# One-by-one release of row scatters, and a new order of loads, ranks and clears, in an attention and expert-layer kernel

## The chip, the cores and the metric

The kernel runs on one core of one Trainium2 chip. The metric is the device time of one execution, in microseconds (us). The core's engines are TensorE (PE, matrix products, with its weight loads shown as PEld), VectorE (DVE), ScalarE (ACT), GpSimd (POOL) and SyncE (SP, which issues most DMA transfers). Each works through its own queue of instructions in order, and semaphores tie the queues together.

## The reference

Linear attention with decay over batch 4, 8 heads, 768 positions, 64 values per head, and then a layer of 8 experts of which each row uses one:

```python
intra = (q_block @ k_block.T) * Dmask      # per block of positions
inter = (q_block * lam_pow) @ kv_state
kv_state = lam_block * kv_state + (k_block * rev_pow).T @ v_block
x = attn_out.transpose(0, 2, 1, 3).reshape(B * S, H * D)     # 3072 rows of 512
logits = x @ w_gate + modality_bias[modality_id]
e_idx = argmax(logits)                     # one expert for each row
h = relu(x[mask] @ w1[e])                  # 512 to 1024
out[mask] = gate_w[mask] * (h @ w2[e])     # 1024 to 512
```

All data is float32. With these inputs the rows go to four of the eight experts: 1319 to expert 3, 1494 to expert 6, 253 to expert 5 and 6 to expert 7.

## The kernel before

**Attention.** The kernel walks the positions in 24 blocks of 128, taken in 12 pairs m = 0 to 11 (a pair's data, 2048 KB, is one `load`). For a block, `scores` are matmuls of keys and queries (L251), `mask` multiplies them by the decay on DVE (L256), `keys` makes the decayed keys `kd` on ACT (L233, for the first two blocks on POOL), `query` makes `qd` on POOL (L218), `products` multiply `kd` with the values (L264), `add` brings them into the state on DVE (L274), `from_state` multiplies `qd` with the state (L286), and `values` adds the masked scores times the values (L294) and copies the sum to `xt` on ACT (L298). `scores` and `keys` of a pair are made ahead, in the iteration before it. After every second pair `turns` transposes four blocks' results into rows (L312 on PE, L316 on DVE, L318 on ACT) and `gates` makes the logits (L323).

**Routing.** The 24 blocks form three batches of eight. `choose` finds each row's expert on DVE, `ranks` (L375 to L378, PE) counts the rows ahead of it, `slots_of` turns that into a place, and for each block `one_slot` copies its tags (L406) and scatters the 128 rows into a DRAM table `placed` (L407, both on POOL). `count` (L436) and the lists of tiles follow, in DVE operations that are queued up by `put` (all at L348) and emitted by `do`, between other work. Scatters wait in a list of `jobs`. `go` issues some at a given place, `tick` issues one that waits for a given matmul to finish, and `need` issues what is left. In the attention part the table `aside` says how many are issued in pairs 6, 7, 8, 10 and 11, at two places each; from the second tile on `first_layer` and `second` call `tick` on their matmuls.

**Experts.** The rows are fetched back in tiles of 256 (tiles 0 to 3 from lists that are made early, then a tile of 64 and one of 32 rows, then eight further full ones; nine more are conditional and are not run with these inputs). A matrix is split into a high part (ACT, L596) and a low part (DVE, L597) and a product is the sum of three matmuls (L693 to L695). `first_layer` makes `hh` and `hl`, `second` the output, which ACT scales (L741) and POOL scatters to the result (L744). The low parts `w2l` of a tile are made during its own `first_layer`. The two small tiles use unsplit products (`thin_first`, L765) and turn the result (`thin_turn`, L776). The weights of the second of them are loaded into tiles of their own, `both1` and `both2`; other weights go to `raw1` and `raw2`. Rows past the end of an expert's part of `placed` are cleared by `clear_end` on SP, in two DMAs for each expert, of 64 rows always and of 192 rows if needed (two of the eight are, here).

**What sets the order.** PE, DVE, ACT and SP run their instructions in the order of the code; on POOL the order is tied together by `pool`. SP issues in that order too, and a load waits there until its target is free, so what stands behind it waits as well.

Of the kernel before, what the change touches and what calls it, by code (L numbers as in the profile page):

```python
# [15 lines left out]
P = 128  # L16
# [27 lines left out]
def linear_attention_moe(tc, qkv, lam, modality, wg, mbias, w1, w2, out):  # L44
    nc = tc.nc
    with ExitStack() as ctx:
# [28 lines left out]
        nc.scalar.dma_start(out=lamh, in_=lam.rearrange("h o -> (h o)").partition_broadcast(P))  # L75
# [170 lines left out]
        def scores(g):  # L246
            kt, qt, vt, kn = loaded(g)
            scs[g] = ps.tile([P, 2, NP, P], F32, name="s", bufs=2)
            for p in range(NP):
                for hl, r in enumerate(halves2):  # L250
                    mm = nc.tensor.matmul(scs[g][:, hl, p, :], kt[r, p, :], qt[r, p, :], start=True, stop=True)  # L251
                    begun.setdefault(g, mm)

# [35 lines left out]
        def values(g):  # L289
            c = g % NC  # L290
            vt, op, pt = loaded(g)[2], ops.pop(g), pts.pop(g)
            for p in range(NP):
                for hl in range(2):
                    nc.tensor.matmul(op[place(g, hl), p, :], vt[:, (2 * p + hl) * D : (2 * p + hl + 1) * D],  # L294
                                     pt[:, hl, p, :], start=(c == 0 and p == 0), stop=(p == NP - 1))
            if g % 4 == 0:
                xts[g // 4] = work.tile([P, NP, 4, 4, Q], F32, name="xt", bufs=2)
            nc.scalar.copy(out=xts[g // 4][:, :, :, ORDER.index(g % 4), :], in_=op.rearrange("p a (c t) -> p a c t", c=4))  # L298

# [20 lines left out]
        def gates(grp):  # L320
            for p in range(NP):
                for t in range(4):
                    nc.tensor.matmul(lps[t * Q : (t + 1) * Q, grp % 2, :], wgq[:, ORDER[t] % HB, p, :], xts[grp][:, p, :, t, :],  # L323
                                     start=(p == 0), stop=(p == NP - 1), tile_position=(0, t * Q))

        def turns(grp):
            turn(grp, 0)
            turn(grp, 1)
            gates(grp)
            turn(grp, 2)  # L330
            turn(grp, 3)

# [174 lines left out]
        def late_list(exA, nA):  # L507
# [10 lines left out]
            put(nc.vector.tensor_copy, out=ends_at[:, 0, :], in_=beyond)  # L518
# [4 lines left out]
            def first_of(those, nm):  # L523
# [18 lines left out]
            put(nc.vector.scalar_tensor_tensor, out=ends_at[:, 1, :], in0=rem, scalar=0.0, in1=thins, op0=ALU.not_equal,  # L542
                op1=ALU.subtract)
# [92 lines left out]
        def clear_end(e):  # L636
            vr = nc.sync.value_load(ends_at[0:1, 0, e : e + 1], min_val=0, max_val=E * CAP - TT)
            for i in range(2):
                if i == 0:
                    c = clear(bass.ds(vr, XT), XT)  # L640
                else:
                    cr = nc.sync.value_load(ends_at[0:1, 1, e : e + 1], min_val=0, max_val=1)
                    c = clear(bass.ds(vr + XT, TT - XT), TT - XT, cond=cr)
                apart("ends", c)
                for b in range(RN):
                    tc.declare_no_dep(c.ins, group=f"slots{b}", reason="rows differ")
                for b in range(2):
                    tc.declare_no_dep(c.ins, group=f"list{b}", reason="rows differ")
# [76 lines left out]
        behind = []  # L725

        def second(n, t, ticks=(1, 3, 5, 7), hold=False):
# [9 lines left out]
            if hold:  # L737
                y = const.tile([P, DM], F32, name="held")
            else:
                y = work.tile([P, DM], F32, name="y", tag="qd", bufs=4)  # L740
            nc.scalar.activation(out=y, in_=yp, func=AF.Copy, scale=idx[:, t, 1:2].bitcast(F32))  # L741

            def store():
                sc = nc.gpsimd.indirect_dma_start(  # L744
                    out=out, out_offset=bass.IndirectOffsetOnAxis(ap=idx[:, t, 0:1], axis=0),
                    in_=y, in_offset=None, bounds_check=N - 1, oob_is_err=False)
                apart("tokens", sc)
                pool(sc, free=True)

            if hold:  # L750
                behind.append(store)
            else:
                store()
# [60 lines left out]
        ends_at = const.tile([P, 2, E], I32, name="ends_at")  # L814
# [22 lines left out]
        aside = {6: (0, 3), 7: (1, 2), 8: (1, 1), 10: (2, 2), 11: (2, 2)}  # L837

        def block(g, on_pool=False):
            scores(g)  # L840
            mask(g)
            keys(g, on_pool)
            query(g)

# [275 lines left out]
```

## Time and profile before

| | us |
|---|---|
| median of three runs | 424.59 (420.89 to 424.86) |
| profiled execution | 424.69 |
| its span | 423.0 |
| PE busy | 393.4 (93%) |
| DVE busy | 261.9 (62%) |
| ACT busy | 211.1 (50%) |
| POOL busy | 96.8 (23%) |

The span is the profiled stretch; the execution's time holds 1.7 us more. Times in the rows are from the span's start. A timeline row merges instructions of one line that follow each other; "x32" is their number, and the bracket is the idle time before the first of them with what ended it ("issue" is an idle time that nothing in the profile explains).

### The profile page before, as it was taken

What the parts mean: (1) busy time and instruction counts of PE and PEld (TensorE: products, weight loads), DVE (VectorE), ACT (ScalarE), POOL (GpSimd) and SP (SyncE); (2) the same over time, 40 slices, a digit from 0 to 9 for tenths busy, and PEclk for the clock granted to TensorE, in tenths of its full rate; (3) what the DMA queues carried; (4) which work ended last, traced back from release to release, by engine and by line L of the source; (5) the groups of instructions that cost most, each with busy time, mean ns of one, the idle gap of its engine ahead of it and who ended that gap; (6) DMA issues with size and microseconds to landing.
All of it is one profiled execution on the core that took longest, in us unless ns stands there. A gap on an engine that the chain in (4) does not pass through costs nothing.

```text
span 423.0 us, 9783 instructions
## 1 busy us (share of the span) xinstructions
PE 393.4 (93%) x3602; PEld 343.9 (81%) x3602; DVE 261.9 (62%) x478; ACT 211.1 (50%) x411; POOL 96.8 (23%) x126
## 2 busy tenths in 40 slices
PE   6999999896898999999958999999999999999993
PEld 3879888785786888989833899989898989898982
DVE  4557779767468368787221766667666675847530
ACT  1458677574165345555120655464646555546420
POOL 1643217536400167001000102020201010010201
PEclk9999999999798999999997999999999999999998
DMA  6998896989537978125169227787403021210101
GB/s 239 389 404 304 329 339 220 394 272 286 202 101 218 302 265 266 51 53 175 24 173 341 44 51 247 213 242 224 98 24 77 25 51 51 51 51 2 52 2 48
DMA packets 37962, 72.96 MB, mean 172 GB/s; under 512 B 7054, under 2 KB 19854, under 8 KB 37904
## 3 DMA queue, kind: packets, MB, share of 16 engines
q1 hardware_dynamic: 33840, 59.45, 45.2%
q0 software_dynamic: 3920, 12.78, 7.9%
q8 instruction: 30, 0.49, 0.5%
q14 instruction: 28, 0.23, 0.2%
q10 hardware_dynamic: 144, 0.00, 0.0%
HBM read 90.57 MB, written 17.84 MB: 256 GB/s over the span
## 4 chain that ended last, share of the span: by engine, by line
issue 48%; PE 35%; POOL 6%; DVE 5%; DMA 3%; ACT 2%; POOLq 1%; DVEq 0%; ACTq 0%
POOL out_dram L744 5%; PE o L294 5%; PE s L251 5%; PE kv L264 3%; PE o L286 3%; PE o L695 3%; PE o L693 3%; PE o L694 3%; PE o L312 3%; PE s L713 2%; DMA lamh<-in_lam_dram 1%; DVE grp L316 1%; DMA out_dram<-y,idx 1%; PE kv L693 1%; ACT kd L233 1%
## 5 line engine op out<-in xcount | busy, mean ns | idle before, releaser
L597 DVE TENSOR_TENSOR w2l<-raw,w2h 128x1024 fp32r<-128x1024 f32 x48 | 58.8, 1224 | 42.3 <-ACT w2h L596 41.4
L744 POOL DMA_INDIRECT out_dram<-y,idx x23 | 29.1, 1263 | 228.0 <-ACT y L741 228.0
L695 PE MATMUL o<-w2h,hl 128*128 128x512 f32 x192 | 75.6, 394 | 0.0
L693 PE MATMUL o<-w2h,hh 128*128 128x512 f32 x192 | 75.5, 393 | 0.0
L694 PE MATMUL o<-w2l,hh 128*128 128x512 f32 x192 | 75.4, 393 | 0.0
L597 DVE TENSOR_TENSOR w1l<-raw,w1h 128x1024 fp32r<-128x1024 f32 x44 | 51.7, 1220 | 2.4 <-ACT w1h L596 2.3
L695 PE MATMUL kv<-xh,w1l 128*128 128x256 f32 x176 | 50.0, 284 | 0.0
L695 PE MATMUL s<-xh,w1l 128*128 128x256 f32 x176 | 50.0, 284 | 0.0
L596 ACT CAST w2h<-raw 128x1024 fp32r<-128x1024 f32 x48 | 49.9, 1040 | 0.1
L694 PE MATMUL s<-xl,w1h 128*128 128x256 f32 x176 | 49.9, 284 | 0.0
L694 PE MATMUL kv<-xl,w1h 128*128 128x256 f32 x176 | 49.9, 283 | 0.0
L693 PE MATMUL s<-xh,w1h 128*128 128x256 f32 x176 | 49.6, 282 | 0.0
L693 PE MATMUL kv<-xh,w1h 128*128 128x256 f32 x176 | 49.5, 281 | 0.0
L596 ACT CAST w1h<-raw 128x1024 fp32r<-128x1024 f32 x44 | 42.8, 1045 | 0.0
L695 PEld LDWEIGHTS o<-w2h,hl 128*128 128x128 f32 x192 | 36.3, 189 | 7.7
L694 PEld LDWEIGHTS o<-w2l,hh 128*128 128x128 f32 x192 | 36.5, 190 | 7.4
L693 PEld LDWEIGHTS o<-w2h,hh 128*128 128x128 f32 x192 | 36.5, 190 | 7.3
L741 ACT ACTIVATE y<-o,idx 128x512 f32<-128x512 f32 x23 | 15.8, 685 | 43.5 <-PE o L695 37.9
L233 ACT ACTIVATE kd<-load,dk 128x64 f32<-128x64 f32 x144 | 35.5, 336 | 0.1
L218 POOL TENSOR_TENSOR qd<-load,pq 128x512 f32<-128x512 f32 x20 | 25.2, 1276 | 44.3 <-PE s L251 20.5
L693 PEld LDWEIGHTS kv<-xh,w1h 128*128 128x128 f32 x176 | 33.4, 190 | 1.7 <-ACT hh L720 1.7
L693 PEld LDWEIGHTS s<-xh,w1h 128*128 128x128 f32 x176 | 33.3, 189 | 0.6 <-issue 0.2
(208 smaller groups left out, 663.8 us busy)
## 6 DMA issues: line engine op xcount, KB each, us to landing
raw<-in_w_dram SPq DMA_DIRECT2D x104, 512.0 KB
load<-in_qkv_dram SPq DMA_DIRECT2D x9, 2048.0 KB
xg<-placed SPq DMA_DIRECT2D x48, 128.0 KB
load<-in_qkv_dram SPq DMA_DIRECT2D x8, 512.0 KB
both<-in_w_dram SPq DMA_DIRECT2D x8, 512.0 KB
placed<-blank SPq DMA_DIRECT2D x8, 396.0 KB
load<-in_qkv_dram SPq DMA_DIRECT2D x2, 1024.0 KB
placed<-blank SPq DMA_DIRECT2D x8, 132.0 KB
```

The source lines that it names most:

```text
L218: op = pool(nc.gpsimd.tensor_tensor(out=qds[g], in0=loaded(g)[1], in1=pq, op=ALU.mult))
L233: nc.scalar.activation(out=kds[g][:, p, hl, :], in_=kn[:, p, hl, :], func=AF.Copy, scale=dk[:, hl, p, P - 1 : P])
L251: mm = nc.tensor.matmul(scs[g][:, hl, p, :], kt[r, p, :], qt[r, p, :], start=True, stop=True)
L264: nc.tensor.matmul(kp[r, g % HB, p, :], kd[:, p, hl, :], vt[:, (2 * p + hl) * D : (2 * p + hl + 1) * D], start=True, stop=True)
L294: nc.tensor.matmul(op[place(g, hl), p, :], vt[:, (2 * p + hl) * D : (2 * p + hl + 1) * D], pt[:, hl, p, :], start=(c == 0 and p == 0), sto ...
L596: nc.scalar.copy(out=hi, in_=src)
L597: nc.vector.tensor_tensor(out=lo, in0=src, in1=hi.bitcast(F32), op=ALU.subtract)
L693: nc.tensor.matmul(out, ah, bh, start=first, stop=False)
L694: nc.tensor.matmul(out, ah, bl, start=False, stop=False)
L695: return nc.tensor.matmul(out, al, bh, start=False, stop=last)
L741: nc.scalar.activation(out=y, in_=yp, func=AF.Copy, scale=idx[:, t, 1:2].bitcast(F32))
L744: sc = nc.gpsimd.indirect_dma_start(out=out, out_offset=bass.IndirectOffsetOnAxis(ap=idx[:, t, 0:1], axis=0), in_=y, in_offset=None, bound ...
```

## The change

1. `lamh` (the decays) is loaded through SP's queue instead of ACT's.
2. In the first pairs, block 2 is prepared whole, and block 3's keys, before block 1's results; block 4 comes before the turns of group 0, and block 5 between their halves.
3. The scatters of batches one and two no longer use `aside`. From pair 6 on, each of three places (the scores of the pair after next, the values, the gates) calls `tick`; the second batch's jobs start at pair 10 and end on the first tile's matmuls. The first fetch of rows moves from pair 8 to pair 9.
4. The third batch's `ranks` move from ahead of `second(0)` into the first quarter of tile 1's `first_layer`; its scatters, `count` and the late list follow later.
5. `clear_end` makes one DMA of 256 rows for each expert, without a condition.
6. The weights of the first small tile are issued after the clears and after the tile before it (`first_layer`), and `both1` behind the first small tile's rows instead of behind all three fetches.
7. The last output scatter is issued in its place and not behind the conditional tiles.

```diff
-        nc.scalar.dma_start(out=lamh, in_=lam.rearrange("h o -> (h o)").partition_broadcast(P))
+        nc.sync.dma_start(out=lamh, in_=lam.rearrange("h o -> (h o)").partition_broadcast(P))
...
         def clear_end(e):
-            vr = nc.sync.value_load(ends_at[0:1, 0, e : e + 1], min_val=0, max_val=E * CAP - TT)
-            for i in range(2):
-                if i == 0:
-                    c = clear(bass.ds(vr, XT), XT)
-                else:
-                    cr = nc.sync.value_load(ends_at[0:1, 1, e : e + 1], min_val=0, max_val=1)
-                    c = clear(bass.ds(vr + XT, TT - XT), TT - XT, cond=cr)
...
+            vr = nc.sync.value_load(ends_at[0:1, e : e + 1], min_val=0, max_val=E * CAP - TT)
+            c = clear(bass.ds(vr, TT), TT)
...
-            if hold:
-                behind.append(store)
-            else:
-                store()
+            sc = nc.gpsimd.indirect_dma_start(
...
         products(0)
         add(0)
-        scores(2)
-        mask(2)
-        query(2)
+        block(2)
+        keys(3)
         from_state((1,))
         values(1)
         products(1)
-        keys(2)
         add(1)
-        block(3)
+        scores(3)
+        mask(3)
+        query(3)
...
-        turns(0)
         block(4)
+        turn(0, 0)
+        turn(0, 1)
+        gates(0)
         block(5)
+        turn(0, 2)
+        turn(0, 3)
...
                 block(a + 2)
-                block(b + 2)
+                mm = block(b + 2)
+                if m > 5:
+                    tick(mm)
...
-                jobs += [("slots", one_slot)] * RC
...
+            if m == 5 or m == 10:
+                jobs += [("slots", one_slot)] * RC
             do(7)
-            go(aside.get(m, (0, 0))[0])
             from_state((a, b))
-            for g in (a, b):
-                values(g)
+            values(a)
+            mm = values(b)
+            if m > 5:
+                tick(mm)
...
-            go(aside.get(m, (0, 0))[1])
             if m % 2 and ahead:
-                turns(m // 2)
+                mm = turns(m // 2)
+                if m > 5:
+                    tick(mm)
...
                 fetch_w1(*fetch_regs(0, True))
+            elif m == 9:
+                need("slots")
                 fetch_x(0)
-            elif m == 9:
...
         def amid1(i):
             if i == 0:
                 do()
+                ranks(routed[-1])
+                slots += slots_of(*routed)
+            if i < 2:
+                do(4)
+            elif i == 2:
+                do()
                 jobs.extend([("slots", one_slot)] * RC)
-                count()
-                late_list(*early)
-            else:
-                do(4)
...
         first_layer(amid1)
+        count()
+        late_list(*early)
...
         for e in range(E):
             clear_end(e)
-        fetch_w1(*fetch_regs(thins))
+        do()
         for t in range(2):
             second(2, t)
-        do()
...
         first_layer()
-        for n in range(thins, wides + 1):
-            fetch_x(n)
+        fetch_w1(*fetch_regs(thins))
+        fetch_x(thins)
         fetch_w1(*fetch_regs(thins + 1, True), to=both1)
+        fetch_x(thins + 1)
         fetch_w2(*fetch_regs(thins))
+        fetch_x(wides)
         fetch_w2(*fetch_regs(thins + 1, True), to=both2)
```

On POOL, scatters of the first batch in pairs 6 and 7. Before, the next blocks' `qd` stand between groups of copies and scatters, which wait for no matmul (the numbers in brackets are what an instruction waits for):

```order
L407 DMA placed<-grp,sloti 26880x528 [waits Activation_49,Pool_49]
L218 TENSOR_TENSOR qd<-load,pq 128x512 [waits DMAHW4_49,PE_49]
L218 TENSOR_TENSOR qd<-load,pq 128x512 [waits PE_49]
L406 COPY grp<-pay 128x16
L407 DMA placed<-grp,sloti 26880x528 [waits Activation_49,Pool_49]
L406 COPY grp<-pay 128x16
L407 DMA placed<-grp,sloti 26880x528 [waits Activation_49,Pool_49]
L406 COPY grp<-pay 128x16
L407 DMA placed<-grp,sloti 26880x528 [waits Activation_49,Pool_49]
L218 TENSOR_TENSOR qd<-load,pq 128x512 [waits DMAHW5_49,PE_49]
```

Now each scatter waits for PE as well, and `qd` of the following blocks stands behind the scatters that are released before it:

```order
L218 TENSOR_TENSOR qd<-load,pq 128x512 [waits DMAHW4_49,PE_49]
L218 TENSOR_TENSOR qd<-load,pq 128x512 [waits PE_49]
L410 COPY grp<-pay 128x16
L411 DMA placed<-grp,sloti 26880x528 [waits PE_49,Activation_49,Pool_49]
L410 COPY grp<-pay 128x16
L411 DMA placed<-grp,sloti 26880x528 [waits PE_49,Activation_49,Pool_49]
L410 COPY grp<-pay 128x16
L411 DMA placed<-grp,sloti 26880x528 [waits PE_49,Activation_49,Pool_49]
L218 TENSOR_TENSOR qd<-load,pq 128x512 [waits DMAHW5_49,PE_49]
L410 COPY grp<-pay 128x16
L411 DMA placed<-grp,sloti 26880x528 [waits PE_49,Activation_49,Pool_49]
```

What moved is the release: a scatter starts no longer when POOL is free but when its matmul is done. The second batch's eight stand in one row in both kernels, and gain the same wait.

On PE, the passage from tile 0's first layer (L713, later L710) to its second. Before, the ranks stand between the two; the piece has the last matmuls of the first layer and the first of the ranks, then the last rank and the first of the second layer:

```order
L713 MATMUL kv_1902<-xt2_127,raw1_1390 128x256 [waits DMAHW3_49,DVE_49]
L713 MATMUL kv_1902<-xt2_127,raw1_1390 128x256 x7
L375 LDWEIGHTS lowb_106
L375 MATMUL x_124<-oh_1897,lowb_106 128x64 [waits DVE_49]
L376 LDWEIGHTS onesb_105
L376 MATMUL x_124<-ohsum_125,onesb_105 128x64
```

```order
L378 LDWEIGHTS onesb_105
L378 MATMUL x_124<-oh_1897,onesb_105 128x8
L693 MATMUL o_2034<-w2h_1789,hh0_1793 128x512 [waits PE_49,Activation_49]
L694 MATMUL o_2034<-w2l_1790,hh0_1793 128x512
L695 MATMUL o_2034<-w2h_1789,hl0_1795 128x512
```

Now the second layer follows at once, and the ranks (L379) stand behind the first quarter of the next tile's first layer:

```order
L710 MATMUL s_1874<-xt2_127,raw1_1388 128x256 x7
L710 MATMUL kv_1902<-xt2_127,raw1_1388 128x256 [waits DMAHW3_49,DVE_49]
L710 MATMUL kv_1902<-xt2_127,raw1_1388 128x256 x7
L690 MATMUL o_2015<-w2h_1777,hh0_1781 128x512 [waits DVE_49,Activation_49]
L691 MATMUL o_2015<-w2l_1778,hh0_1781 128x512
L692 MATMUL o_2015<-w2h_1777,hl0_1783 128x512
```

```order
L691 MATMUL s_2075<-xl1_131,w1h_1779 128x256
L692 MATMUL s_2075<-xh1_129,w1l_1780 128x256
L379 LDWEIGHTS lowb_106
L379 MATMUL x_124<-oh_1897,lowb_106 128x64
L380 LDWEIGHTS onesb_105
```

What moved is the wait on DVE: the first rank no longer has one here.

On SP, the end of the fetches that precede `both`. Before, the rows of the first wide tile (`xg`) and their tags stand ahead of it:

```order
L615 DMA xg<-placed 32x8x128
L615 ISA
L615 DMA xg<-placed 32x8x128
L619 ISA
L619 DMA idx_3009<-placed 128x2x2
L664 TENSOR_LOAD listC
L664 ISA x2
L672 ISA
L672 DMA both_2854<-in_w_dram 128x1024
```

Now the tags of the first small tile (`idx`) stand ahead of it, and the first wide tile's rows come after:

```order
L617 ISA
L617 DMA xq_2893<-placed 32x2x128
L624 ISA
L624 DMA idx_2892<-placed 64x2
L624 ISA
L624 DMA idx_2892<-placed 64x2
L661 TENSOR_LOAD listC
L661 ISA x2
L669 ISA
L669 DMA both_2751<-in_w_dram 128x1024
```

What moved is `both`, ahead of the fetch of the second small tile and of the first wide tile.

## Rows read from the trace of the kernel before

**Rows 1.** Page: busy us (share of the span) of each engine; GB/s in 40 equal slices.

```profile
PE 393.4 (93%) x3602; PEld 343.9 (81%) x3602; DVE 261.9 (62%) x478; ACT 211.1 (50%) x411; POOL 96.8 (23%) x126
...
GB/s 239 389 404 304 329 339 220 394 272 286 202 101 218 302 265 266 51 53 175 24 173 341 44 51 247 213 242 224 98 24 77 25 51 51 51 51 2 52 2 48
```

**Rows 2.** Waits of PE: who waited for whom: us in total, times, longest.

```profile
PE s L765 <- DMA both<-in_w_dram: 5.9, 3, 5.5
PE o L286 <- issue: 5.7, 3, 5.1
...
PE x L375 <- DVE oh L348: 1.9, 1, 1.9
...
PE x L436 <- DVE ohsum L348: 1.5, 1, 1.5
```

**Rows 3.** Windows view: stretch, length, busy us of PE, PEld, DVE, ACT, POOL, clock, DMA.

```profile
237.00:416.00 179.00, 179.00 (x1152) 163.79 (x1151) 114.25 (x123) 94.92 (x124) 21.28 (x16) 1.00 0.31 88
```

**Rows 4.** Timeline of ACT, then of PE, 16 to 32 us.

```profile
16.46 3.94 ACT L233 ACTIVATE kd<-load,dk 128x64 f32<-128x64 f32 x16
...
17.42 3.37 PE L264 MATMUL kv<-load,kd 128*64 128x64 f32 x32
...
25.03 1.07 PE L312 MATMUL o<-ident,xt 128*128 128x128 f32 x8 [0.78 <-ACT xt L298]
...
30.27 1.91 PE L264 MATMUL kv<-load,kd 128*64 128x64 f32 x16
```

**Rows 5.** Windows (pairs m = 5 and m = 7), then timeline of PE and DVE at 74 to 77.

```profile
52.75:62.21 9.46, 9.46 (x187) 8.30 (x187) 6.61 (x18) 6.55 (x24) 1.28 (x1) 1.00 0.92 324
68.16:80.46 12.30, 10.37 (x161) 8.35 (x161) 8.79 (x32) 4.84 (x16) 8.41 (x12) 1.00 0.98 350
...
74.32 0.63 PE L264 MATMUL kv<-load,kd 128*64 128x64 f32 x16
...
77.00 0.85 DVE L274 SCALAR_TENSOR_TENSOR state<-state,pq,kv 128x64 f32<-128x64 f32 x4 [2.21 <-PE o L312]
```

**Rows 6.** Timeline of DVE, PE, POOL at 93 to 107, and the stretch 104 to 112.

```profile
93.31 0.86 DVE L274 SCALAR_TENSOR_TENSOR state<-state,pq,kv 128x64 f32<-128x64 f32 x4 [1.48 <-PE kv L264]
...
101.60 0.63 PE L264 MATMUL kv<-load,kd 128*64 128x64 f32 x16
...
103.60 0.21 DVE L348 TENSOR_TENSOR deltaB<-deltaB,ntB 128x8 f32<-128x8 f32 x1
107.30 0.85 DVE L274 SCALAR_TENSOR_TENSOR state<-state,pq,kv 128x64 f32<-128x64 f32 x4 [3.49 <-remote]
...
105.08 0.98 POOL L407 DMA_INDIRECT placed<-grp,sloti  x1 [0.28 <-issue]
...
106.55 0.98 POOL L407 DMA_INDIRECT placed<-grp,sloti  x1 [0.28 <-issue]
...
104.00:112.00 8.00, 4.28 (x52) 3.98 (x54) 3.31 (x13) 0.00 (x0) 6.29 (x11) 0.57 0.87 282
```

**Rows 7.** Windows view, the stretch behind the third batch's ranks.

```profile
132.00:136.00 4.00, 4.00 (x12) 3.14 (x12) 3.09 (x5) 3.15 (x5) 0.00 (x0) 0.57 0.82 259
```

**Rows 8.** Timeline of SP, PE and ACT at the small tiles; a window of the clears.

```profile
181.13 19.83 SPq L633 DMA_DIRECT2D placed<-blank  x16
...
218.01 1.96 SPq L672 DMA_DIRECT2D both<-in_w_dram  x4
...
213.50 3.67 PE L765 MATMUL s<-raw,xf 128*64 128x256 f32 x32
...
228.92 0.66 PE L776 MATMUL x<-ident,hn 128*128 128x128 f32 x4
...
220.59 1.14 ACT L596 CAST xh<-xt 128x512 fp32r<-128x512 f32 x2 [6.30 <-DVE xt L681]
...
196.00:198.00 2.00, 2.00 (x19) 2.00 (x18) 1.28 (x2) 1.02 (x2) 0.00 (x0) 1.00 0.84 240
```

**Rows 9.** Chain that ended last: start, us, what.

```profile
412.18 4.23 DMA out_dram<-y,idx
```

More of the change, by code (lines that the diff above doesn't have):

```diff
@@ L293, in values @@
                 for hl in range(2):
-                    nc.tensor.matmul(op[place(g, hl), p, :], vt[:, (2 * p + hl) * D : (2 * p + hl + 1) * D],
-                                     pt[:, hl, p, :], start=(c == 0 and p == 0), stop=(p == NP - 1))
+                    mm = nc.tensor.matmul(op[place(g, hl), p, :], vt[:, (2 * p + hl) * D : (2 * p + hl + 1) * D],
+                                          pt[:, hl, p, :], start=(c == 0 and p == 0), stop=(p == NP - 1))
             if g % 4 == 0:
@@ L322, in gates @@
                 for t in range(4):
-                    nc.tensor.matmul(lps[t * Q : (t + 1) * Q, grp % 2, :], wgq[:, ORDER[t] % HB, p, :], xts[grp][:, p, :, t, :],
-                                     start=(p == 0), stop=(p == NP - 1), tile_position=(0, t * Q))
+                    mm = nc.tensor.matmul(lps[t * Q : (t + 1) * Q, grp % 2, :], wgq[:, ORDER[t] % HB, p, :], xts[grp][:, p, :, t, :],
+                                          start=(p == 0), stop=(p == NP - 1), tile_position=(0, t * Q))
+            return mm
         def turns(grp):
@@ L328, in turns @@
             turn(grp, 1)
-            gates(grp)
+            mm = gates(grp)
             turn(grp, 2)
             turn(grp, 3)
+            return mm
         shape = [P, RC, E]
@@ L636, in clear_end @@
         def clear_end(e):
-            vr = nc.sync.value_load(ends_at[0:1, 0, e : e + 1], min_val=0, max_val=E * CAP - TT)
-            for i in range(2):
-                if i == 0:
-                    c = clear(bass.ds(vr, XT), XT)
-                else:
-                    cr = nc.sync.value_load(ends_at[0:1, 1, e : e + 1], min_val=0, max_val=1)
-                    c = clear(bass.ds(vr + XT, TT - XT), TT - XT, cond=cr)
[L644 to L648, printed above, removed]
+            vr = nc.sync.value_load(ends_at[0:1, e : e + 1], min_val=0, max_val=E * CAP - TT)
+            c = clear(bass.ds(vr, TT), TT)
+            apart("ends", c)
+            for b in range(RN):
+                tc.declare_no_dep(c.ins, group=f"slots{b}", reason="rows differ")
+            for b in range(2):
+                tc.declare_no_dep(c.ins, group=f"list{b}", reason="rows differ")
         def thin_rows(n):
@@ L723, in first_layer, with second @@
                 between(i)
-        behind = []
-        def second(n, t, ticks=(1, 3, 5, 7), hold=False):
+        def second(n, t, ticks=(1, 3, 5, 7)):
             idx = idxs[n]
@@ L736, in second @@
                     tick(mm)
-            if hold:
-                y = const.tile([P, DM], F32, name="held")
-            else:
-                y = work.tile([P, DM], F32, name="y", tag="qd", bufs=4)
+            y = work.tile([P, DM], F32, name="y", tag="qd", bufs=4)
             nc.scalar.activation(out=y, in_=yp, func=AF.Copy, scale=idx[:, t, 1:2].bitcast(F32))
[L743 to L750, printed above, removed]
-                behind.append(store)
-            else:
-                store()
+            sc = nc.gpsimd.indirect_dma_start(
+                out=out, out_offset=bass.IndirectOffsetOnAxis(ap=idx[:, t, 0:1], axis=0),
+                in_=y, in_offset=None, bounds_check=N - 1, oob_is_err=False)
+            apart("tokens", sc)
+            pool(sc, free=True)
         def thin_first(x, w):
@@ L836, in linear_attention_moe @@
         pairs = B * NC // HB
-        aside = {6: (0, 3), 7: (1, 2), 8: (1, 1), 10: (2, 2), 11: (2, 2)}
         def block(g, on_pool=False):
-            scores(g)
+            mm = scores(g)
             mask(g)
@@ L977, in linear_attention_moe @@
         fetch_x(2)
-        ranks(routed[-1])
         turn_rows(1)
         split_rows()
-        slots += slots_of(*routed)
-        split_w1(1)
+        split_w1()
         fetch_w1(*fetch_regs(2))
@@ L1048, in linear_attention_moe @@
             for t in range(2):
-                second(n, t, hold=n + 1 == fixed_ones and t == 1)
+                second(n, t)
         ordered.close()
@@ L1064, in linear_attention_moe @@
                     second(n, t)
-        for store in behind:
-            store()
 _INS = ["qkv", "lam", "modality", "wg", "mbias", "w1", "w2"]
```

11 lines of the change are left out of this document (6 added, 5 removed).

## The prediction, made before the result was known

> **What bounds the kernel now.** I read the page's busy table first. TensorE (PE) is busy for 393.4 of 423.0 us [rows 1], so at most 29.6 us can come from its idle time, and a little more from matmuls that run at the lower clock. The view of waits, for PE, says where the large gaps are [rows 2]: 5.9 us for the weights of the small tiles (`both`), 5.7 us in three gaps before the matmuls from the state (L286), 1.9 us before the third batch's ranks (L375) and 1.5 us before a count (L436). Then I read the timeline around each, for what ended the wait. From 237 to 416 us, where the wide tiles run, the windows view shows PE busy 179.00 of 179.00 us [rows 3]: whatever is gained ahead of that arrives later only as an earlier start, and reaches the end whole.
>
> A measurement of this kernel tells about 1% (some 4 us) from no change. The sum is made against the profiled execution's own time, 424.69 us (1.7 us beyond its span), 0.1 above the median of 424.59.
>
> **First blocks.** Two blocks' `kd` on ScalarE (ACT) take 3.94 us for 16 instructions from 16.46, and the 32 products that read them take 3.37 us from 17.42: PE goes at ACT's pace [rows 4]. Sixteen products that nothing paces take 0.63 us, as those at 74.32 do [rows 5], so 32 take at most 1.26 and 2.1 us is lost. The 16 products at 30.27 take 1.91, again beside `kd`: 1.3 lost. The turn at 25.03 waits 0.78 for ACT's copy [rows 4]. Together 4.2 us. The new order issues kd(2), kd(3), kd(4) and kd(5) while PE has other work. I take 3.6 of the 4.2, since block 5's `kd` still stands near its use; bounds 2.5 and 4.5. The cover is the load: four pairs of 2.10 MB each with 0.2 MB of constants are 8.6 MB, and by the page's slices of 10.575 us at 239, 389 and 404 GB/s [rows 1] 6.6 MB has come by 21.2 us and 8.6 MB by about 26. Blocks 6 and 7, whose scores stand behind the 30.27 products at 32.1, thus have about 6 us of room: the gain is not swallowed. `lamh` on SP's queue instead of ACT's changes who issues it first: I take 0, bounds −0.5 and +0.4 (one issue, against SP having to issue it ahead of the loads).
>
> **Scatters of the first batch (m = 6 to 8).** In before, three scatters stand in a row behind the `turns` of pair m = 7's work. The products there end at 74.95, the state's update on VectorE (DVE) starts at 77.00, though its operands are there. That pair took 12.30 us where an odd pair without scatters took 9.46: 2.84 lost [rows 5]. Released one per half-pair, a scatter has its hand-over behind it. Three places a pair remain and each may still touch one hand-over, so I take 2.5; bounds 1 and 4 (the latter with what m = 8 loses).
>
> **Scatters of the second batch (m = 10, 11).** Products end at 102.23, DVE's list work at 103.81, and the update starts only at 107.30, while scatters of 0.98 us run with 0.28 us between them. Where no scatter runs, the update at 93.31 starts when its products end [rows 6]. After the change two scatters remain in this stretch and the other six move into the first tile's layer, whose matmuls wait for no such update. The update then starts behind DVE's list work at 103.9: 3.4 us gained, 1.5 us of stall left. [...]
>
> The row says that a hand-over from PE to DVE beside scatters takes 107.30 − 102.23 = 5.07 us, of which 1.58 is DVE's own list. [...]
>
> **Ranks and count of the third batch.** The ranks wait 1.9 us for DVE's `oh` ahead of `second(0)` [rows 2]. Then `second(0)` begins, and in the four us from 132 PE is busy throughout at a granted clock of 0.57 [rows 7]: 4.00 × 0.43 = 1.7 us lost. In the new place, behind the first quarter of tile 1's layer, `oh` is many us old. I gain 1.9 + 1.7 = 3.6, bounds 2.5 and 3.8. The count's 1.5 us wait on `ohsum` goes the same way: after `first_layer(1)` the DVE sums lie three steps back. I take 1.5, bounds 0.5 and 1.6. What is late next: `late_list` puts more small DVE operations (0.16 to 0.25 us each, as the one at 103.60) ahead of tile 3's layer. Some 12 of them are about 2 us on DVE, hidden because the first reader of `w2l` is `second(3)`; without that cover they cost those 2 us. The last scatters of this batch now come with `second(1)`, and the fetch of tile 3 needs only the lists' rows.
>
> **Clears and small tiles.** Before, 16 clear instructions keep SP from 181.13 to 200.96. `both` is issued at 218.01, PE ends the first small tile's layer at 217.17 and then waits for it, and the transposes at 228.92 come last. Now there are 8 clears: about half of 19.83, so SP is through at 191. They move 8 × 541 KB = 4.3 MB instead of two such and six of 135 KB. The DMA row of 196 to 198 shows 240 GB/s at a share of 0.84, or 285 GB/s full: 15.2 us, so the last byte is in by 198 [rows 8]. The first small tile's fetch waits for that, `both` is issued 3 to 6 us behind, at about 203, and its 2 MB need 7.4 us at 285 GB/s: there by 212, five before PE wants it. PE would then end the second layer at 217.17 + 3.67 = 220.8. The fetch of the first wide tile, now behind one more weight group, lands about as before, so ACT's two casts of it still run from 220.59 to 221.73, ahead of the small tile's `hn`. That one is as large as one cast, 0.57: the small tile's transposes start at about 222.4 instead of 228.92, 6.5 gained. I take 5.5, since x, weights and the last clear share the DMA engines; bounds 4 (`both` 2 us late) and 8.1 (transposes at 220.8).
>
> **End.** The last output scatter was held back behind the conditional tiles; now it is issued in its place. Its 4.23 us to landing [rows 9] remain, and what stands behind it (branches, POOL's closing row) may come before or after. I take −0.5; bounds −1.2 and +0.5.
>
> Sum: 3.6 + 2.5 + 5.5 + 3.6 + 1.5 + 5.5 − 0.5 = 21.7. 424.69 − 21.7 = 403.0 us.
>
> **Rivals.**
> A. The bunching is not the cause, or one scatter holds a hand-over as much as six: the 2.5 and 5.5 stay lost. For it: three places a pair still stand beside updates. Against it: the update at 93.31. Time 403.0 + 8.0 = 411.0. [...]
> B. The clears' 4.3 MB, in 2 KB rows, drain slower than the 285 GB/s, and the small tile's fetch comes no sooner, so `both` is no earlier. For it: clears of 135 KB are rated here beside weights, not alone. Against it: the DMA share was 0.84 with a 396 KB clear running. The small tiles bring 0 to 1: time 407.5 to 408.5.
> C. Slower: a scatter that waits for a matmul makes PE's queue answer for it, so that each of the 24 costs PE a full scatter cycle (1.47 us from one start to the next, 105.08 to 106.55 [rows 6]) at the matmul that releases it. [...] For it: POOL's order is fixed, so a `qd` behind a waiting scatter waits too. Against it: `qd` is read a pair later, and PE itself waits for no scatter here.
>
> **Chances.** Forecast 0.68 (its own range 397 to 407); A 0.12; B 0.12; C 0.03; 0.05 for less than 397, where terms reach their upper bounds. The range from 396 to 412 takes in A and B. Faster by over 1% 0.93; within 1% 0.04 (A and B together with a poor start); slower 0.03.
>
> **What would show it.** Right: the update behind the products of m = 11 starts within 2 us of their end; no PE wait at ranks and count; no half clock at those two places; `both` issued before 206 and no PE wait for it; transposes of the small tile 5 to 6 us nearer the first small layer's start than 15.4; all wides gapless. Wrong: updates that start over 2 us late beside single scatters (A); clears that end after 203 (B); gaps at the releasing matmuls (C); a new wait for a load among the first eight blocks.

## The result, and the profile after

The changed kernel takes 401.79 us (median of four runs, 401.10 to 402.31) where the kernel before took 422.74 on the same chip: a ratio of 0.9503, 95% interval 0.9438 to 0.9568. The profiled run took 402.04 us with a span of 400.3.

The page's first part and the waits of PE, of the kernel after. They answer to [rows 1, 2]: PE is busy 11.9 us less with the same 3602 matmuls (clock given back, 0.993 granted in the mean against 0.975, products that wait less for `kd`, and 1.1 us in the wide tiles). Three of the four large gaps are gone, and the fourth, ahead of the matmuls from the state, has fallen from 5.7 to 3.6 us. A new one stands on top, before the small tile's transposes (L761).

```profile
span 400.3 us, 9742 instructions
...
PE 381.5 (95%) x3602; PEld 336.9 (84%) x3602; DVE 263.3 (66%) x477; ACT 210.7 (53%) x411; POOL 100.2 (25%) x126
```

```profile
PE x L761 <- ACT hn L754: 3.8, 1, 3.8
PE o L287 <- DVE state L275: 3.6, 2, 2.1
PE o L777 <- DVE hnt L763: 1.4, 2, 0.8
PE o L808 <- DVE busy L99: 1.3, 1, 1.3
PE s L251 <- DMA load<-in_qkv_dram: 1.2, 3, 0.5
```

By the starts of PE's matmuls in the timelines, the 22.65 us of span divide so (a stage ends where the next begins; m counts iterations over pairs):

| stage | before | after | gain | predicted |
|---|---|---|---|---|
| start to the scores of block 6 | 32.11 | 27.66 | 4.45 | 3.6 |
| m = 2 to 6, scores of blocks 6 to 15 | 35.97 | 35.97 | 0 | 0 |
| m = 7 and 8 | 18.93 | 17.86 | 1.07 | 2.5 |
| m = 9 | 9.66 | 9.66 | 0 | 0 |
| m = 10 and 11, to tile 0's first layer | 15.89 | 10.34 | 5.55 | 5.5 |
| tiles 0 and 1 (ranks, count) | 55.97 | 50.43 | 5.54 | 5.1 |
| to the first small layer | 44.97 | 44.70 | 0.27 | 0 |
| small tiles, to the first wide tile | 23.50 | 19.00 | 4.50 | 5.5 |
| wide tiles | 179.62 | 178.56 | 1.06 | 0 |
| end | 6.36 | 6.14 | 0.22 | −0.5 |

PE's timeline after, in three stretches. The first answers to [rows 4]: the products of block 4 now take 0.69 us, at nobody's pace; those of blocks 2 and 3 take 1.74, where 32 that nothing paces take 1.10 (as at 32.47). At 68.13 a wait of 2.09 us stands that was not foreseen. At 98.57 the hand-over of m = 11 costs the 1.50 us that were foreseen, against 5.12 in the kernel before (the second piece).

```profile
16.05 1.74 PE L265 MATMUL kv<-load,kd 128*64 128x64 f32 x32
...
26.42 0.69 PE L265 MATMUL kv<-load,kd 128*64 128x64 f32 x16
27.66 2.06 PE L251 MATMUL s<-load 64*128 64x128 f32 x32 [0.55 <-DMA load<-in_qkv_dram]
...
68.13 1.09 PE L287 MATMUL o<-qd,state 64*64 64x128 f32 x28 [2.09 <-DVE state L275]
...
96.07 0.63 PE L265 MATMUL kv<-load,kd 128*64 128x64 f32 x16
...
98.57 1.09 PE L287 MATMUL o<-qd,state 64*64 64x128 f32 x28 [1.50 <-DVE state L275]
```

```profile
107.72 1.97 PE L286 MATMUL o<-qd,state 64*64 64x128 f32 x28 [5.12 <-issue]
```

The windows view of the first stretch of tile 0's second layer, and of the wide tiles. The clock is 1.00 where it was 0.57 [rows 7], and the wides are gapless as in [rows 3].

```profile
118.00:122.00 4.00, 4.00 (x20) 3.32 (x18) 3.69 (x9) 1.07 (x3) 0.00 (x0) 1.00 0.88 291
```

```profile
216.00:394.00 178.00, 178.00 (x1152) 162.70 (x1150) 113.88 (x123) 94.54 (x124) 21.26 (x16) 1.00 0.30 88
```

### The profile page after: what moved, and what is told of

It reads as the page before. It is cut to its first block, busy times and chain, and to the rows that moved or that the text cites. A ratio compares the mean times of both kernels' runs of the same rounds, so it can differ in the third digit from the quotient of the medians.

```text
span 400.3 us, 9742 instructions
## 1 busy us (share of the span) xinstructions
PE 381.5 (95%) x3602; PEld 336.9 (84%) x3602; DVE 263.3 (66%) x477; ACT 210.7 (53%) x411; POOL 100.2 (25%) x126
## 4 chain that ended last, share of the span: by engine, by line
issue 49%; PE 26%; DVE 7%; DMA 6%; POOL 6%; SPq 3%; ACT 1%; POOLq 0%; DVEq 0%; ACTq 0%
POOL out_dram L734 5%; DMA load<-in_qkv_dram 5%; PE o L295 3%; PE s L251 3%; PE o L690 2%; PE o L692 2%; PE o L287 2%; PE o L691 2%; PE s L710 2%; PE kv L710 2%; DVE pt L257 2%; PE o L314 2%; DVE state L275 1%; PE kv L265 1%; SPq L639 1%
## 5 line engine op out<-in xcount | busy, mean ns | idle before, releaser
L734 POOL DMA_INDIRECT out_dram<-y,idx x24 | 31.4, 1308 | 204.0 <-ACT y L733 203.4
L218 POOL TENSOR_TENSOR qd<-load,pq 128x512 f32<-128x512 f32 x20 | 25.2, 1277 | 35.1 <-PE s L251 27.6
L691 PEld LDWEIGHTS s<-xl,w1h 128*128 128x128 f32 x176 | 33.2, 188 | 0.4
```

Source lines behind the costliest of these rows:

```text
L218: op = pool(nc.gpsimd.tensor_tensor(out=qds[g], in0=loaded(g)[1], in1=pq, op=ALU.mult))
L691: nc.tensor.matmul(out, ah, bl, start=False, stop=False)
L734: sc = nc.gpsimd.indirect_dma_start(out=out, out_offset=bass.IndirectOffsetOnAxis(ap=idx[:, t, 0:1], axis=0), in_=y, in_offset=None, bound ...
```

## The experiments

Stages of all profiles, in us, from the same starts of PE's matmuls, with the median and the ratio to the kernel before on the same chip. The kernel before took 418.4 us on the chip of the first group (bunched, lam_act, hn_first, list_six), 424.0 on that of the second (before_again to thin_free) and 425.4 on that of the third.

| kernel | start | m = 7, 8 | m = 10, 11 | tiles 0, 1 | small tiles | median | ratio |
|---|---|---|---|---|---|---|---|
| before | 32.11 | 18.93 | 15.89 | 55.97 | 23.50 | 422.7 | |
| after | 27.66 | 17.86 | 10.34 | 50.43 | 19.00 | 401.8 | 0.950 |
| bunched | 27.73 | 15.43 | 10.41 | 50.46 | 19.78 | 400.9 | 0.961 |
| lam_act | 30.70 | 19.03 | 10.34 | 50.46 | 20.82 | 407.4 | 0.975 |
| hn_first | 27.63 | 19.30 | 10.34 | 50.47 | 17.59 | 402.1 | 0.962 |
| list_six | 27.61 | 18.47 | 10.34 | 50.47 | 20.81 | 404.2 | 0.968 |
| before_again | 33.84 | 17.82 | 14.76 | 56.10 | 23.02 | 424.7 | 1.002 |
| after_again | 27.73 | 15.40 | 10.34 | 50.47 | 20.60 | 402.7 | 0.951 |
| lam_only | 30.75 | 17.49 | 13.96 | 56.14 | 23.23 | 420.5 | 0.991 |
| thin_free | 28.73 | 17.50 | 14.02 | 50.47 | 22.27 | 410.7 | 0.966 |
| bunched_again | 27.65 | 17.35 | 15.08 | 50.46 | 20.91 | 408.0 | 0.959 |
| ranks_clears | 27.64 | 15.70 | 10.34 | 54.37 | 27.70 | 413.9 | 0.974 |
| first_sp | 30.81 | 16.23 | 10.35 | 50.47 | 16.16 | 401.5 | 0.946 |
| tuned | 27.69 | 15.56 | 10.34 | 50.46 | 21.21 | 407.9 | 0.958 |

**Are grouped scatters the cause? (bunched, bunched_again)** The changed kernel with the scatters issued in groups again, those of the second batch from pair 9 on as before:

```diff
-                mm = block(b + 2)
-                if m > 5:
-                    tick(mm)
+                block(b + 2)
...
+            go(aside.get(m, (0, 0))[0])
```

> The changed kernel with the scatters of batches one and two issued in the old groups again (the table aside; 3 to 4 in a row), all else as after. If bunched scatters hold the hand-over from PE to DVE, the state's update of m = 11 starts some 5 us after the products' end, the clock falls behind it, pair 7 takes about 12 us, and the time is 401.8 + 5.5 + 1.1 = 408.4 us. If the scatters were not the cause (another part of the change took the stall away), the time stays within 1.5 us of 401.8 and the update starts within 2 us.

Measured: 0.9607 (0.9553 to 0.9660), and no loss: m = 10 and 11 take 10.41 us with the scatters of m = 11 in one row, and m = 7 and 8 are 2.4 shorter than in after. By this run rival A would have stood. But the kernel before was over 4 us faster on this chip too (418.4 against 422.7), so the same kernel ran again elsewhere.

> The kernel with grouped scatters a second time, unchanged. Theory: what grouped scatters cost is not fixed by the program but by whether semaphore traffic is slow beside them in that run: where the kernel before takes about 424 us on this chip, the stretch from the scores of pair 11 (block 22) to the first tile's layer is about 14 us here against 10.3 with single release, and the time 404 to 406; where before takes 415 to 419, the stretch is 10.4 and the time 401, as in the first run. Rival: grouped scatters never cost anything in the new kernel (the 14 us of the other kernel came from its moved loads): 10.4 and 401 whatever before takes.

Measured: 0.9589 (0.9522 to 0.9656), and m = 10 and 11 take 15.08. DVE's and PE's timelines of this run at m = 11: the products end at 96.60, DVE's list at 97.77, and the update starts only at 99.64; PE waits 3.11, and then the clock is halved (the windows row, 0.50).

```profile
97.56 0.21 DVE L352 TENSOR_TENSOR deltaB<-deltaB,ntB 128x8 f32<-128x8 f32 x1
99.64 0.85 DVE L275 SCALAR_TENSOR_TENSOR state<-state,pq,kv 128x64 f32<-128x64 f32 x4 [1.87 <-remote]
```

```profile
100.07 1.97 PE L287 MATMUL o<-qd,state 64*64 64x128 f32 x28 [3.11 <-issue]
```

```profile
98.80:105.50 6.70, 5.43 (x60) 4.83 (x60) 3.13 (x13) 0.58 (x1) 5.03 (x9) 0.50 0.85 290
```

The same program, in the first run: the update follows DVE's list at once, beside the same scatters.

```profile
95.72 0.21 DVE L352 TENSOR_TENSOR deltaB<-deltaB,ntB 128x8 f32<-128x8 f32 x1
95.85 0.84 DVE L275 SCALAR_TENSOR_TENSOR state<-state,pq,kv 128x64 f32<-128x64 f32 x4
```

So the expectation's theory holds for the stage, though the time is 2 us above the 406 that it allowed. Grouped scatters cost 3.6 to 5.5 us in m = 10 and 11 (13.96 to 15.89 against 10.34) wherever the kernel before took 423 to 426, and nothing in the one profile where it took 418. With single release the stage took 10.34 or 10.35 us in all eight profiles, on every chip. In m = 7 and 8 of the chip of the first group, single release cost 3.0 to 3.9 us (18.47 to 19.30 against 15.43), so that there rival A stands; on the other two chips it gained 1.1 to 2.4 (15.40 to 16.23 against 17.35 to 17.82). Why the hand-over is late on some chips stays open.

**The two kernels again (before_again, after_again)**, both unchanged.

> The kernel before, unchanged, for a second profile. Theory: the late update of m = 11 (5 us after the products) and the 12.3 us of pair 7 belong to the kernel, and stand in this profile too. Rival: they belong to the one profiled execution or to its state of the core (the kernel's times spread from 415 to 425 us); then the update starts within 2 us of the products and pair 7 takes under 11 us, with a time of 415 to 418.

> The changed kernel, unchanged, on the same chip as the next two. Both theories: first scores at 5.6 us, the 2.1 us wait of PE in pair 6 with DVE's multiply of 2.67 us beside qd; 0.950 to 0.965 of the kernel before. It is the reference for the kernel with grouped scatters: if grouped scatters are the better, this is 2 us slower than that one was (0.9607).

Measured: 424.65 and 402.71 us; before_again equals before (1.0016, 0.9994 to 1.0039), after_again is at 0.9513 (0.9454 to 0.9572). The stall of m = 11 is there again (14.76), and m = 7 takes 11.44 against an expected 12.3, so the theory holds with a smaller stall. after_again did not show the 2.1 us wait of m = 7: that part of the expectation failed. The two profiles of the same program, DVE then POOL, first after, then after_again:

```profile
65.12 2.67 DVE L352 TENSOR_TENSOR pastA<-pastA,deltaA 128x16 f32<-128x16 f32 x1
...
65.26 2.49 POOL L218 TENSOR_TENSOR qd<-load,pq 128x512 f32<-128x512 f32 x2
```

```profile
65.19 0.17 DVE L352 TENSOR_TENSOR pastA<-pastA,deltaA 128x16 f32<-128x16 f32 x1
65.28 1.61 DVE L275 SCALAR_TENSOR_TENSOR state<-state,pq,kv 128x64 f32<-128x64 f32 x8
...
65.56 2.51 POOL L218 TENSOR_TENSOR qd<-load,pq 128x512 f32<-128x512 f32 x2 [0.41 <-PE s L251]
```

The small DVE multiply, which reads two tiles of SBUF, took 0.17 us in after_again, where it was over before `qd` began, and 2.67 in after, where it ended at 67.79 and `qd` at 67.75. With grouped scatters three of them stand ahead of this `qd`, and it starts at 66.71 (POOL's row of bunched, below), behind DVE's list. With single release only two do: the third waits for the scores, which are those of the next pair and not of the pair after next, as the list of changes has it. So `qd` starts sooner, where DVE's list is not over or has just ended: at 65.26 in after, 0.14 us behind the multiply's start, and at 65.56 in after_again, 0.20 behind its end. The hold stands in all three profiles of the first group's chip that have single release and in after, and in none of after_again, ranks_clears and first_sp.

```profile
66.71 2.54 POOL L218 TENSOR_TENSOR qd<-load,pq 128x512 f32<-128x512 f32 x2
```

**Can the list be moved out of the way? (list_six)**

```diff
-            do(7)
+            do(6 if m == 6 else 7)
```

> The changed kernel with one DVE list operation fewer in pair 6 (the multiply that took 2.67 us beside POOL's qd; it goes to pair 7). Theory: that operation was held until qd ended, and the 2.1 us PE wait before L287 at 68.1 is its doing: the update starts by 65.9, time 401.8 - 2.0 = 399.8. Rival: the update itself is held by qd just so (or waits for something else), it starts at 67.7 as before and the time stays 401.8.

Measured: 404.2 us, m = 7 and 8 at 18.47: the time of neither. The operation two places earlier met `qd` and took 3.15 us, and the update followed at 68.00, when `qd` was over. In lam_act and hn_first, whose list has all seven operations, it is that earlier one too (2.99 and 3.08 us): on this chip the operation that was taken away was not the one held. The update itself is not held where it runs beside `qd`: it takes 1.61 us so in after_again, and 1.62 alone in list_six. To take one operation away was not enough: two different ones, each reading two tiles, were held.

```profile
64.73 3.15 DVE L352 TENSOR_TENSOR pastA<-sidx,sumsEA 128x16 f32<-128x16 f32 x1
67.92 0.17 DVE L352 TENSOR_REDUCE exA<-pastA 128x2 f32<-128x16 f32 x1
68.00 1.62 DVE L275 SCALAR_TENSOR_TENSOR state<-state,pq,kv 128x64 f32<-128x64 f32 x8
```

**`lamh` on one queue or the other (lam_act, lam_only).** after with ACT's queue, and before with SP's:

```diff
-        nc.sync.dma_start(out=lamh, in_=lam.rearrange("h o -> (h o)").partition_broadcast(P))
+        nc.scalar.dma_start(out=lamh, in_=lam.rearrange("h o -> (h o)").partition_broadcast(P))
```

> The changed kernel with lamh loaded through ACT's queue again. Theory: the 1.4 to 1.7 us by which the first blocks start sooner come from lamh; first scores at 6.9 us instead of 5.6, time 401.8 + 1.5 = 403.3. Rival: the start of the first loads varies from run to run and lamh has no part; first scores at about 5.6, time 401.8.

> The kernel before with lamh on SP's queue, nothing else. Theory: lamh ahead of the loads on one queue brings the first scores from 7.0 to 5.6 us and the masks with them: 1.4 to 3 us less than before. Rival: lamh matters only with the new order of blocks: no change within 0.5 us.

Measured: lam_act 407.4 us, 0.975, start 30.70 against 27.6 to 27.7, so twice the 1.5 us that its theory had; lam_only 420.5 us, 0.9907 (0.9870 to 0.9944), start 30.75 against 32.11 and 33.84. In the timelines of DVE and PE, first of before, then of lam_only, both the decays and the first loads come sooner:

```profile
5.71 2.63 DVE L118 TENSOR_TENSOR_SCAN dk<-lamh,anti 128x128 f32<-128x128 f32 x8 [4.33 <-DMA lamh<-in_lam_dram]
...
6.96 1.16 PE L251 MATMUL s<-load 64*128 64x128 f32 x16 [1.66 <-DMA load<-in_qkv_dram]
```

```profile
3.73 2.63 DVE L118 TENSOR_TENSOR_SCAN dk<-lamh,anti 128x128 f32<-128x128 f32 x8 [2.35 <-DMA lamh<-in_lam_dram]
...
5.63 1.16 PE L251 MATMUL s<-load 64*128 64x128 f32 x16 [0.76 <-DMA load<-in_qkv_dram]
```

So this line alone is worth 1.4 to 3.1 us at the start, in either order of blocks. The 1.4 is before against lam_only. In lam_act and before_again the first matmuls are slow as well: sixteen that take 1.16 us in before take 2.08 in lam_act and 1.47 in before_again. With `lamh` on SP's queue thin_free has them too (2.08, and a start of 28.73), so what goes beyond 1.4 is not the load's alone.

```profile
7.81 2.08 PE L251 MATMUL s<-load 64*128 64x128 f32 x16 [2.50 <-DMA load<-in_qkv_dram]
```

**Ranks, count and the two-part clears where they were (ranks_clears)**, in the changed kernel:

```diff
+        ranks(routed[-1])
         turn_rows(1)
...
+                    cr = nc.sync.value_load(ends_at[0:1, 1, e : e + 1], min_val=0, max_val=1)
+                    c = clear(bass.ds(vr + XT, TT - XT), TT - XT, cond=cr)
```

> The changed kernel with the third batch's ranks, places, count and late list where they were before, and with the clears in two parts, the second under a condition. Theory: the ranks wait 1.9 us with a half clock behind it, the count 1.5: from the first tile's layer to the second layer of tile 1 some 5.6 us more; the clears cost nothing more, since both1 has 5 us to spare, or up to 1 us. Time 402.5 + 5.6 = 408 us. Rival: the sixteen clears keep SP some 9 us longer, both1 comes 4 us late and PE waits for it: 412 us.

Measured: 413.9 us. Tiles 0 and 1 take 54.37, 3.94 more: the two waits are back, 1.9 and 1.5. Before's 55.97 is 1.6 longer still, with a granted clock of 0.57 behind the first wait [rows 7]. On the clears the rival (412 us) is right, and more than right: the small tiles take 27.70. The clears start 32.4 us ahead of the first small layer, as after's do (32.0), so this loss is not the ranks'. PE's two waits, then SP and PE from the clears on:

```profile
PE x L379 <- DVE oh L352: 1.9, 1, 1.9
PE x L440 <- DVE ohsum L352: 1.5, 1, 1.5
```

```profile
166.29 19.87 SPq L637 DMA_DIRECT2D placed<-blank  x16
...
194.55 1.97 SPq L676 DMA_DIRECT2D both<-in_w_dram  x4
...
207.76 1.89 SPq L619 DMA_DIRECT2D xg<-placed  x4
```

```profile
204.95 3.38 PE L757 MATMUL s<-both,xf 128*32 128x256 f32 x32 [2.62 <-issue]
215.42 1.11 PE L768 MATMUL x<-ident,hn 128*128 128x128 f32 x4 [7.09 <-ACT hn L761]
```

**The old first blocks and the old order of SP's fetches, with the eight clears (first_sp):**

```diff
-        fetch_w1(*fetch_regs(thins + 1, True), to=both1)
-        fetch_x(thins + 1)
-        fetch_w2(*fetch_regs(thins))
-        fetch_x(wides)
+        for n in range(thins, wides + 1):
+            fetch_x(n)
+        fetch_w1(*fetch_regs(thins + 1, True), to=both1)
+        fetch_w2(*fetch_regs(thins))
```

> The changed kernel with the first blocks in their old order and SP's fetches of the small tiles in theirs. Theory: PE reaches blocks 6 and 7 some 3 us later (the load gain stays), and waits 4 to 5.5 us for both1: 402.5 + 3 + 4.5 = 410 us. Rival: with eight clears alone SP is early enough, both1 comes in time in the old order as well, and only the 3 us of the first blocks are lost: 405.5.

Measured: 401.47 us, 0.9456 (0.9375 to 0.9537), 4 us under the rival's time and 8.5 under the theory's. The start is 3.1 us later, as both expected. The small tiles take 16.16, less than any other: the old order of fetches is the better one once the clears are eight. SP, ACT and PE, of after and then of first_sp:

```profile
164.63 10.20 SPq L635 DMA_DIRECT2D placed<-blank  x8
...
185.82 1.98 SPq L669 DMA_DIRECT2D both<-in_w_dram  x4
...
197.90 1.93 SPq L617 DMA_DIRECT2D xg<-placed  x4
...
204.32 1.14 ACT L598 CAST xh<-xt 128x512 fp32r<-128x512 f32 x2 [6.90 <-DVE xt L678]
205.37 0.86 ACT L754 ACTIVATE hn<-s 128x512 f32<-128x512 f32 x2
...
206.01 0.65 PE L761 MATMUL x<-ident,hn 128*128 128x128 f32 x4 [3.84 <-ACT hn L754]
```

```profile
191.97 1.87 SPq L617 DMA_DIRECT2D xg<-placed  x4
...
195.44 1.96 SPq L669 DMA_DIRECT2D both<-in_w_dram  x4
...
198.89 1.12 ACT L598 CAST xh<-xt 128x512 fp32r<-128x512 f32 x2
201.94 0.60 ACT L754 ACTIVATE hn<-s 128x512 f32<-128x512 f32 x1 [1.93 <-PE s L750]
...
206.30 0.66 PE L761 MATMUL x<-ident,hn 128*128 128x128 f32 x4
```

In first_sp the wide tile's rows (`xg`) are issued 6.2 us ahead of the first small layer's start and in after 1.3 behind it, ACT casts them before `hn` is due, and PE pays 1.4 us in two short waits for `both`. In after `both` is early and `xg` late, and `hn` waits behind its casts for 3.8 us; after that wait the granted clock is 0.50 from 207.30 to 210.60, and in first_sp it is 1.00 from 198 to 215. The first small tile's second layer and the windows view of that stretch, of after; with the clock at 1.00 those 32 matmuls take 3.67 us (first_sp, at 207.74):

```profile
207.45 5.22 PE L777 MATMUL o<-raw,hnt 128*64 128x256 f32 x32 [0.79 <-DVE hnt L763]
```

```profile
207.30:210.60 3.30, 3.15 (x16) 1.82 (x18) 0.09 (x1) 0.00 (x0) 0.00 (x0) 0.50 1.05 295
```

**Freeing `hn` by other means (hn_first, thin_free, tuned).** hn_first moves the wide tile's transposes and splits behind the small tile's turn:

```diff
-        turn_rows(wides)
-        split_rows()
         fetch_x(wides + 1)
...
         hnt = thin_turn(hns[0])
+        turn_rows(wides)
+        split_rows()
```

> The changed kernel with the first wide tile's transposes and splits (DVE, ACT) moved behind the small tile's hn and its turn. Theory: the 3.8 us wait of PE before the small tile's transposes is ACT's queue alone (hn behind the casts of the wide tile); the transposes follow the second small layer within 0.5 us, no half clock there, time 401.8 - 4 = 398 us. Rival: the small tile's second weights (raw2, issued at 195.7) land only at about 204 to 206 and take the place of the wait: gain 0 to 1.5, time 400.3 to 401.8.

Measured: 402.1 us. The transposes follow the second small layer at once, so the wait was ACT's queue, as the theory has it. The small tiles take 17.59, but PE then waits 2.9 us for the second tile's second weights, and the half clock reaches into the first wide tile (0.50 from 213.2 to 220 us); the wide tiles take 2.1 us longer. About the rival's time (400.3 to 401.8), by a transfer one further than it named.

thin_free adds grouped scatters and fetches those weights ahead of the wide tile's rows; tuned has single release, that order too, `raw2` ahead of the second tile's rows, and moves the first list behind the turns of m = 7:

```diff
-        fetch_x(wides)
         fetch_w2(*fetch_regs(thins + 1, True), to=both2)
+        fetch_x(wides)
```

> The changed kernel with three edits: scatters of the first two batches grouped as before (table aside), the first wide tile's transposes and splits behind the small tile's hn and turn, and both2's fetch ahead of the first wide tile's rows. Theory: the small tiles' stage has no DMA wait left, from the end of the second small layer to the first wide tile it takes 11 us instead of 15.4, and the first two batches take 2.4 us less: 401.8 - 6 = 396 us or 0.94 of before. Rival: the first wide tile's rows are now late (its first layer waits for xh), or the half clock moves into the wide tile, and the small tiles give back what they gained: as the kernel with grouped scatters, 0.96 of before.

> The changed kernel with two edits: the first list's DVE operations leave pair 6 and the middle of pair 7 (none stands beside qd there; they follow the turns of pair 7), and in the small tiles' stage the first tile's second weights are fetched ahead of the second tile's rows, both2 ahead of the first wide tile's rows, and that tile's transposes and splits follow the small tile's turn. Theory: pairs 6 to 7 take 9.6 us as in the second profile of after, and from the second small layer to the first wide tile 11.5 us instead of 15.4 to 17: 398 us, 0.94 of before. Rival: DMA is the bound of that stage (8 MB of weights), the wait moves to both2 or to the wide tile's weights, and the half clock with it: 401 to 403.

Measured: 410.7 and 407.9 us, where 396 and 398 were expected. thin_free is worse than after on its chip (402.7), and tuned no better than after by the ratio (0.958 against 0.950 and 0.951). Both pay in the same place, with the wide tile's rows late as the rival of thin_free says: `xg` is now last, DVE stands at its transposes (7.06 us in tuned), and the small tile's second turn (`hnt`) waits behind them for 7.7 and 6.7 us. In tuned the later list also pushed the choice of experts beside a `qd`; the second batch's ranks waited 2.6 us, and m = 9 took 15.55 instead of 9.66.

## Why the prediction was right, and where its terms were not

The time (403.0 against 401.8) held, and so did the mechanism of the larger terms. That the sum came so near is luck in part: first blocks, ranks, wide tiles and end brought 0.9, 0.4, 1.1 and 0.7 us more than foreseen, the first batch and the small tiles 1.4 and 1.0 less. It is luck of the chip as well: where grouped scatters cost nothing, the term of the second batch is nothing. The sum starts from an execution of 424.69; by the medians (422.74 and 401.79) the gain is 20.95.

*First blocks.* Predicted 3.6 for the order and 0 for `lamh`; measured 3.1 for the order (first_sp) and 1.4 to 3.1 for `lamh` (lam_only), 1.4 where the first sixteen scores take 1.16 us in both (before and lam_only). The step that failed is `lamh`: "I take 0, bounds −0.5 and +0.4". The issue was counted, not that the decays wait for this load (4.33 us in before, 2.35 in lam_only) and that it lands beside ten others. The cover named (the loads) has gone: block 6's scores now wait 0.55 us for theirs.

*Second batch of scatters.* 5.55 against 5.5, with the 1.5 us of stall foreseen. Of the 5.5, 3.4 is the stall gained; no run shows the 2.1 beyond it as a term of its own. What the traces show in its place is a granted clock of 0.57 from 104 to 112 us in before and of 1.00 from 98 to 104 in after, and the last 28 matmuls from the state and the 32 of the values behind them, which took 4.83 us before (107.72 to 112.55) and 2.92 after (98.57 to 101.49): 1.9 less. The mechanism is shown where grouped and single release ran on the same chip: 13.96 to 15.89 against 10.34. On one chip grouped scatters cost nothing, so the term belongs to the chip as well as to the program.

*First batch.* 1.07 against 2.5. "each may still touch one hand-over" is not what happened: with one scatter fewer ahead of it, `qd` starts where DVE's list stands, and in four of the seven profiles whose list stands there (after, lam_act, hn_first, list_six) a list operation was held for 2.7 to 3.2 us. Without that meeting the term is 2.4 (before_again against after_again).

*Ranks and count.* 5.54 against 5.1: 3.9 with the ranks and the count where they were (ranks_clears; 3.4 of it the two waits) and 1.6 more in before, taken as the clock's part, an estimate (the granted clock was 0.57 there over 4 us [rows 7]), against 3.4 and 1.7.

*Small tiles.* 4.50 against 5.5. The chain up to the transposes held. Counted from the first small layer's start, SP is through with the clears 21.8 us ahead of it (22.5 foreseen), `both` is issued 10.8 us ahead (about 10.5), PE does not wait for it, `xg` is issued 1.3 us behind (0.3 in before, so "about as before"), and the transposes come 9.4 us behind it where they came 15.4: 6.0 nearer, of the 6.5 worked out. What the sum left out stands behind them: PE still waits 3.84 us for `hn`, the clock is at 0.50 after it, and the first small tile's second layer takes 5.22 us instead of 3.67. Nor did the sum part the clears from the order of fetches. The runs do: eight clears instead of sixteen are worth some 7 to 9 us in either order (19.0 to 20.9 against 27.70, and 16.16 against 23.0 to 23.5), and with eight the new order costs 2.8 to 4.4 us (16.16 against after and after_again).

*End.* +0.2 against −0.5: the two paths are level, and all profiles of both kernels have 6.0 to 6.4 us there. C is gone: no gap stands at a releasing matmul. B's slow clears are gone too: SP has issued them by 174.8, and from 180 to 182 us, ahead of the first small tile's fetch at 181.3, DMA moves nothing (0 GB/s).

A kernel with the change but the old order of the small tiles' fetches was not run. From first_sp less the 3.1 us of its first blocks it would be at some 398 us, an estimate from those two rows.

## What to carry to other kernels

When a load is put earlier in a queue, ask what is put later by it, and which in-order engine then stands at the late one: here every reorder of four fetches moved the wait to one that came late (`xg`: 3.8 us in after, 7.7 in thin_free, 6.7 in tuned). A shorter instruction stream on the issuing queue (eight clears that move more bytes, for sixteen that move less) was worth more here than any order (some 7 to 9 us against 2.8 to 4.4). Judge a wait between engines from more than one profile and chip before building on it, and after tying an instruction of one engine to another's, look at what now runs beside it.

## What the runs showed that was not expected

- In after, lam_act, hn_first and list_six a DVE operation with two inputs in SBUF met POOL's `qd` and ended 0.03 to 0.05 us behind it: 0.17 us became 2.67 to 3.15. What starts the hold was not shown: in the four profiles with the hold DVE's operation is recorded 0.14 to 0.6 us ahead of `qd`, while a scatter still runs on POOL, and in after_again an operation that started so, beside a scatter, took 0.17. In tuned an addition of `choose` that began 0.12 us behind `qd` took 2.48 us and ended 0.10 behind it.
- Beside grouped scatters the hand-over from PE to DVE was late past DVE's own list by 3.5 us in before and 1.9 in bunched_again, and not at all in bunched, the same program as bunched_again on another chip.
- With the small load on a second queue the first scores, which wait for the first large load, came 1.4 to 2.2 us later (7.0 to 7.8 in before, before_again and lam_act against 5.6 in after and lam_only; 6.2 in thin_free), although SP issued the large loads 0.5 us sooner (0.83 against 1.30).
- The wide tiles, gapless at a granted clock of 1.00 in before and after, take 179.6 to 179.8 us in the four profiles whose `ends_at` has two rows, and 178.6 to 178.7 in seven of the ten where it has one. The two-part clears go with the second row in these same kernels; neither the row (32 bytes) nor the clears were tried alone, and the cause stays open.
